# Turning gates in 32x32 blocks on VectorE, and slot sums over 32 tokens in sixteen parts of the array

## The chip, the cores and the metric

The kernel runs on one core of a Trainium2 chip. The metric is the device time of one execution, in microseconds, as the median of several runs. The core has TensorE (PE, matmuls into PSUM), VectorE (DVE), ScalarE (ACT), GpSimd (POOL) and SyncE (SP, which issues the DMAs).

## The reference

Three blocks follow each other. Talking-heads attention (4 batches, 12 heads, 448 tokens, 64 per head) gives `x` of 1792 tokens by 768. A feed-forward block with a gate follows, and a soft mixture of 8 experts with 4 slots each, 32 slots in all:

```
h = x @ w_in                    # 1792 x 2048
x = (h - tanh(h)) @ w_out       # the gated values g, then 1792 x 768
logits = x @ phi                # 1792 x 32
d = exp(logits - logits.max(0)); d /= d.sum(0) + 1e-09
slot_input = d.T @ x            # 32 x 768, then two matmuls per expert
...
c = exp(logits - logits.max(1)); c /= c.sum(1, keepdims=True) + 1e-09
out = c @ slot_out
```

## The kernel before

The kernel never forms `g @ w_out`. The logits are `g @ (w_out @ phi)`, with the product of the two weights (`wphi`) made once, and the slot inputs are `(d.T @ g) @ w_out`: a sum over tokens of `g`, 32 slots by 2048 features, which then goes through `w_out`. That sum over tokens is the place of the change.

The tokens come in four passes of 512, 512, 512 and 256 (`PASS`), the features in 16 blocks of 128, so there are 64 steps `t`, with `b, f = divmod(t, 16)`. A step computes one tile of `h` transposed, 128 features by 512 (or 256) tokens: 18 matmuls into one of three PSUM banks (`product`, L755), with the weights of `w_in` as the stationary side, split into a high and a low part. While TensorE computes step `t`, the other engines gate tile `t-1`: ScalarE squares it (`sq`), squares again (`qd`), takes tanh (`g`) and a mask (`mk`); VectorE forms `h - tanh(h)`, and where `h` is small replaces it by a polynomial in `qd` and `sq` (L786 to L800). `sq` lies in a PSUM bank.

The gated tile has features on the partitions. The sum over tokens needs tokens there, so TensorE turns it: `turn_g` (L826) makes four 128x128 transposes into PSUM, two steps after the product, and ScalarE copies the result (L829) into one of five SBUF buffers of 8 KB per partition (`tq`, `quad`). At the fourth to sixth step of the next pass, the softmax weights of the 32 slots for the pass (`et`, 32 slots in each of four copies) are turned in the same way (`slot_turn`, L946), and `slot_sum` (L958) contracts over 128 tokens at a time: 16 matmuls of 32 slots by 512 features, four of them side by side in the four 32-column parts of the array, half in one step and half in the next. A running sum `SA` (128 x 512) is rescaled and added to (L966).

Nothing is scheduled by a compiler. The order on each engine is the order in which the program issues instructions: `step` puts hooks between the matmuls of a product (`on(c, fn)` calls `fn` before the matmuls of contraction block `c`, `KD` after the last), and each engine goes through its own list in order, waiting on semaphores.

In the last pass the high part of a weight tile is made in two halves by VectorE (L714) and ScalarE (L716), and GpSimd subtracts it from the whole for the low part (L717). From the second pass on, SyncE loads expert weights (1536 KB each) into every buffer that comes free (`give`, `load_expert`). Behind the last step comes the tail: softmax and slot sum of the last pass, `dt` (L1152, the slot sums turned and scaled), `si` (times `w_out`, L1163), and the experts (`h`, `tz`, `so`).

Of the kernel before, what the change touches and what calls it, by code (L numbers as in the profile page):

```python
# [566 lines left out]
def moe_and_slots(tc, ident, xd, wi, wo, wo4, wis, consts, w1, w2, out, box):  # L567
# [23 lines left out]
    XW = KD * TM  # L591
    RU = 2 * DM
# [18 lines left out]
    def r32(ap):  # L611
        return ap.bitcast(F32R)
# [9 lines left out]
    quad, quad_a, quad_b = [xep.tile([128, FB * NRM], FP32, tag=f"quad{i}", name="quad") for i in range(3)]  # L622
# [120 lines left out]
    hps, quads, tok = {}, {}, {}  # L743
# [26 lines left out]
    def gate_act(t, beside=None):  # L770
        hp = hps[t]
        if t > 1:
            mem["sq"] = {t: bank(f"q{t % 2}", [128, PASS[t // NF]], "sq")}
        sq, qd, mk, g = temps_of(t)
        nc.scalar.activation(out=sq, in_=hp, func=ACTF.Square)  # L775
        nc.scalar.activation(out=qd, in_=sq, func=ACTF.Square, bias=tshift)
        if t >= LAST:
            gate_poly(t)
        if beside:
            beside()  # L780
        nc.scalar.activation(out=g, in_=hp, func=ACTF.Tanh)
        nc.scalar.activation(out=mk, in_=sq, func=ACTF.Relu, bias=tlimit, scale=-1.0)  # L782
# [6 lines left out]
    def gate_first(t):  # L789
        hp = hps[t]  # L790
        sq, qd, mk, g = temps_of(t)
        if t < LAST:
            gate_poly(t)
        nc.vector.tensor_tensor(out=g, in0=hp, in1=g, op=ALU.subtract)
# [17 lines left out]
    def turn_bank(shape, name):  # L812
        if mem.get("sum") is not None:
            return bank("r0", shape, name)
        turns[0] += 1
        return bank(f"r{turns[0] % 2}", shape, name)

    def turn_g(t):
        b, f = divmod(t, NF)
        n = blocks[b]  # L820
        if f % NG == 0:
            tok[b, f // NG] = place(b, f // NG)
        g = g_of(t)
        x = turn_bank([128, n, 128], "gt")
        for r in range(n):
            nc.tensor.transpose(out=x[:, r, :], in_=g[:, r * 128:(r + 1) * 128], identity=ident)  # L826
        i = f % NG
        dst = tok[b, f // NG].rearrange("p (r f) -> p r f", r=n)[:, :, i * 128:(i + 1) * 128]
        nc.scalar.activation(out=dst, in_=x, func=ACTF.Copy)  # L829

    def place(b, k):
        if b == NPASS - 1:
            n = blocks[b] * FB
            return quads["C" if k < 2 else "D"][:, k % 2 * n:(k % 2 + 1) * n]
        return quads["AECDB"[(b * NQ + k) % 5]]
# [105 lines left out]
    def slot_turn(b):  # L941
        a, et = es_in[b]
        n = blocks[b]
        xe = turn_bank([128, n, NSL], "etp")
        for r in range(n):
            nc.tensor.transpose(out=xe[:, r, :], in_=et[:NSL, r * 128:(r + 1) * 128], identity=ident[:NSL, :NSL])  # L946
        es = keep.tile([128, NRM, NSL], FP32, tag="es", name="es")
        nc.scalar.activation(out=es[:, :n], in_=xe, func=ACTF.Copy)
        es_in[b] = (a, es)

    def slot_sum(b, lo, hi):
        a, es = es_in[b]
        if lo == 0:
            mem["sum"] = bank("r1", [128, FB], "sp")
        x = mem["sum"]
        for r in range(lo, hi):
            for k in range(NQ):
# [3 lines left out]
        if hi < blocks[b]:  # L961
            return
        mem["sum"] = None
        s = mem["SA"][:, :FB]
        if b:
            nc.vector.scalar_tensor_tensor(out=s, in0=s, scalar=a, in1=x, op0=ALU.mult, op1=ALU.add)  # L966
        else:
            nc.vector.tensor_copy(out=s, in_=x)
# [7 lines left out]
    def step(t):  # L976
# [14 lines left out]
        if t > 2:  # L991
            split_half(t + 1, 0)
            gate_act(t - 1, lambda: split_half(t + 1, 1) if t >= NF else split_w(t + 1, nc.gpsimd))
        else:
            split_w(t + 1, nc.gpsimd)
# [6 lines left out]
        on(4 if t > LAST + 2 else 2, turn_g, u)  # L1002
# [98 lines left out]
    mem["mk"] = tmp.tile([128, TM], FP32, tag="mk", name="mk")  # L1101
    mem["wo"] = [mem["ex"][0][:, i * DM:(i + 1) * DM] for i in range(NG)]
# [3 lines left out]
    quads.update(A=quad_a, B=quad_b, C=tq[:, :FB * NRM], D=tq[:, FB * NRM:], E=quad)  # L1106
# [29 lines left out]
    give(tmp.tile([128, EXB], FP32, tag="tz", name="ex"))  # L1136
    mix_t(b)
# [11 lines left out]
    nc.vector.tensor_scalar(out=sr, in0=ident, scalar1=rv, scalar2=None, op0=ALU.mult)  # L1149
    dt = bank("h2", [128, NG, 128], "dt")  # L1150
# [256 lines left out]
```

## Time and profile before

| | |
|---|---|
| time, median of 3 runs | 930.33 us (929.08 to 930.88) |
| profiled execution | 929.89 us, of which the span of the trace is 928.2 us |
| mean granted TensorE clock | 0.988 of 2.4 GHz |
| busy: PE, DVE, ACT, POOL | 97%, 61%, 62%, 32% of the span |
| attention, then the 64 steps | to about 485 us, then to 818 us |
| tail | 818 to 928 us |

Busy shares are unions of the times in which an engine had an instruction. Matmuls overlap in the pipeline, so one lasts longer than the distance from its start to the next one's start. One FP32 matmul is recorded as two instructions (x2); a matmul on fp32r data (`hp`) or a transpose is one. The chain of waits follows the work that ended last back to the start, and what stands on it adds up to the span.

### The profile page before, as it was taken

The numbers are of one execution on the slowest core, as the hardware profiler recorded it, in microseconds if no ns is written. First come the engines' busy times: TensorE is split into PE (matmuls) and PEld (weight loads), VectorE is DVE, ScalarE is ACT, GpSimd is POOL, SyncE is SP. The second block draws the span as 40 slices with busy tenths as digits, with TensorE's granted clock in tenths as the row PEclk, the third lists the DMA queues.
The fourth block names the chain that finished last, engine by engine and source line by source line (L and its number), as shares of the span: only waits on it lengthen the run. The fifth ranks groups of instructions, "written<-read, shape, count | busy, mean of one in ns | idle before, by whom it ended". The sixth has DMA issues, their size and how long they took to land.

```text
span 928.2 us, 19426 instructions
## 1 busy us (share of the span) xinstructions
PE 898.9 (97%) x6926; PEld 659.8 (71%) x6926; DVE 564.2 (61%) x1267; ACT 574.0 (62%) x1299; POOL 296.5 (32%) x499
## 2 busy tenths in 40 slices
PE   8999999999999999999999999999999999999995
PEld 6667777777777777777777777767776776874542
DVE  3576667767577676786555567567766776740104
ACT  4776767777677777777666576646664665730113
POOL 1464445644456444565432222000000014610000
PEclk9999999999999999999999999999999999998997
DMA  6988688976889567674467868769764445879997
GB/s 134 241 219 234 190 242 226 235 216 200 230 233 267 179 201 215 205 249 145 144 238 246 324 232 269 257 243 365 290 226 157 155 131 187 314 297 425 422 389 279
DMA packets 143988, 223.95 MB, mean 241 GB/s; under 512 B 60756, under 2 KB 125332, under 8 KB 140052
## 3 DMA queue, kind: packets, MB, share of 16 engines
q1 hardware_dynamic: 140544, 209.83, 70.3%
q10 hardware_dynamic: 3348, 12.87, 3.6%
q8 instruction: 56, 0.92, 0.4%
q14 instruction: 40, 0.33, 0.1%
HBM read 147.96 MB, written 36.18 MB: 198 GB/s over the span
## 4 chain that ended last, share of the span: by engine, by line
PE 90%; DMA 3%; ACT 3%; DVE 2%; issue 1%; POOL 0%; ACTq 0%; POOLq 0%; SPq 0%; DVEq 0%
PE hp L755 24%; PE pm L297 15%; PE tm L333 14%; PE vx L357 8%; PE sc L266 7%; PE h L1195 3%; DMA D<-S 3%; PE gt L826 3%; PE so L1234 2%; PE tz L1213 2%; PE lgp L876 2%; PE sp L958 1%; PE wt L845 1%; PE qx L245 1%; PE wp L857 1%
## 5 line engine op out<-in xcount | busy, mean ns | idle before, releaser
L333 PEld LDWEIGHTS tm<-wk,e 120*112 120x112 f32 (+1 forms) x1440 | 174.0, 177 | 70.7 <-issue 58.9
L299 DVE TENSOR_REDUCE mx<-pm 120x1 f32<-120x448 f32 x180 | 111.9, 622 | 125.2 <-PE pm L297 124.6
L336 ACT ACTIVATE aT<-tm 112x480 f32<-112x480 f32 x180 | 105.4, 586 | 120.5 <-PE tm L333 120.5
L297 PE MATMUL pm<-D,wpre 120*120 120x448 f32 x360 | 174.2, 566 | 3.8 <-DMA D<-S 2.2
L333 PE MATMUL tm<-wk,e 120*112 120x120 f32 (+1 forms) x1440 | 176.7, 266 | 1.0 <-POOL wk L323 1.0
L323 POOL TENSOR_SCALAR wk<-wpost,rv 120x120 f32<-120x120 f32 x180 | 125.0, 695 | 136.2 <-PE tm L333 115.2
L755 PE MATMUL hp<-xa,rg 128*128 128x512 f32 x576 | 152.5, 405 | 0.0
L755 PEld LDWEIGHTS hp<-xa,rg 128*128 128x128 f32 x576 | 102.4, 188 | 28.5 <-issue 10.7
L306 ACT ACTIVATE e<-pm,mx 120x448 f32<-120x448 f32 x180 | 113.5, 631 | 4.9 <-DVE rv L318 2.3
L717 POOL TENSOR_TENSOR rg<-rg 128x384 fp32r<-128x384 f32 x32 | 32.0, 1013 | 207.9 <-DVE rg L714 193.8
L274 ACT ACTIVATE S<-sc 120x448 f32<-120x448 f32 (+1 forms) x186 | 90.7, 543 | 5.3 <-PE sc L266 3.0
L357 PE MATMUL vx<-aT,vn 112*64 112x120 f32 (+1 forms) x1536 | 84.0, 262 | 0.0
L786 DVE SCALAR_TENSOR_TENSOR qd<-qd,sq 128x512 f32<-128x512 f32 (+1 forms) x62 | 38.3, 617 | 71.6 <-ACT mk L782 63.5
L357 PEld LDWEIGHTS vx<-aT,vn 112*64 112x64 f32 x1536 | 73.9, 137 | 6.2 <-issue 1.1
L775 ACT ACTIVATE sq<-hp 128x512 f32<-128x512 f32 (+1 forms) x62 | 32.9, 530 | 72.6 <-PE hp L755 72.6
L755 PE MATMUL hp<-xb,rg 128*128 128x512 f32 x288 | 74.7, 404 | 0.0
L312 POOL TENSOR_SCALAR rv<-ss 120x1 f32<-120x1 f32 x180 | 43.0, 239 | 96.8 <-ACT e L306 84.6
L297 PEld LDWEIGHTS pm<-D,wpre 120*120 120x120 f32 x360 | 51.4, 182 | 26.4 <-issue 11.4
L266 PE MATMUL sc<-khi,qT 64*120 64x448 f32 (+1 forms) x384 | 68.8, 387 | 0.8 <-DVE qT L249 0.8
L68 POOL TENSOR_TENSOR fa<-fa,f 128x384 f32<-128x384 f32 x64 | 65.3, 1020 | 5.3 <-issue 0.3
L755 PEld LDWEIGHTS hp<-xb,rg 128*128 128x128 f32 x288 | 52.0, 188 | 16.6 <-issue 6.3
L708 POOL TENSOR_TENSOR rg<-rg 128x768 fp32r<-128x768 f32 x13 | 24.0, 1844 | 67.9 <-PE gt L826 33.5
(173 smaller groups left out, 1356.9 us busy)
## 6 DMA issues: line engine op xcount, KB each, us to landing
ex<-in_moe_w_dram SPq DMA_DIRECT2D x25, 1536.0 KB
D<-S SPq DMA_DIRECT2D x172, 210.0 KB
rg<-wis SPq DMA_DIRECT2D x32, 768.0 KB
f<-in_moe_w_in_dram SPq DMA_DIRECT2D x32, 384.0 KB
f<-in_moe_w_out_dram SPq DMA_DIRECT2D x32, 384.0 KB
wis<-rg ACTq DMA_DIRECT2D x16, 768.0 KB
rg<-wi SPq DMA_DIRECT2D x26, 384.0 KB
wi<-fa SPq DMA_DIRECT2D x32, 192.0 KB
```

The costliest lines, as they stand in the source:

```text
L68: eng.tensor_tensor(out=out, in0=bits(a), in1=bits(p), op=ALU.add)
L266: nc.tensor.matmul(xs[e][0][:ni], lhsT=qT[n][s, l, p, :ni], rhs=kt[s], start=(i == 0), stop=(i == 2))
L274: nc.scalar.activation(out=dst, in_=xs[e][0][:ni], func=ACTF.Copy)
L297: nc.tensor.matmul(x[:r], lhsT=wpre[:r, :m, :], rhs=D_t.pop(s)[:r], start=True, stop=True)
L299: nc.vector.tensor_reduce(out=mx[:r], in_=x[:r], op=ALU.max, axis=AX.X, negate=True)
L306: nc.scalar.activation(out=e[:r], in_=pp_t.pop(s)[:r], func=ACTF.Exp, bias=mx_t.pop(s)[:r], accum_out=ss[:r])
L312: nc.gpsimd.tensor_scalar(out=rv[:r], in0=ss_t.pop(s)[:r], scalar1=EPS, scalar2=None, op0=ALU.add)
L323: nc.gpsimd.tensor_scalar(out=wk[:r], in0=wpost[:r], scalar1=ss_t.pop(s)[:r], scalar2=None, op0=ALU.mult)
L333: nc.tensor.matmul(x[:, c, :, :m], lhsT=e[:r, c * JP:(c + 1) * JP], rhs=wk[:r, :, :m], start=True, stop=True)
L336: nc.scalar.activation(out=attn_t[n][:, :, :, c0:c0 + m], in_=x[:, :, :, :m], func=ACTF.Copy)
L357: nc.tensor.matmul(x[64 * e:64 * e + 64, i, :ni], lhsT=nat_v[b, h // NP][:, h % NP, c, :], rhs=a[:, c, h, :ni], start=(c == 0), stop=(c == ...
L755: nc.tensor.matmul(hp, lhsT=r32(w[:, m, hl, cs]), rhs=r32(x_of(b, c, l)), start=(c == 0 and i == 0), stop=(c == KD - 1 and i == 2))
```

## The change

`turn_g` no longer uses TensorE, PSUM and ScalarE. VectorE's block transpose turns each 32x32 block of the gated tile in place: partition 32i + l of block tb holds, after it, token 32 tb + l for the features 32i to 32i + 31 of the tile. A 512-token tile takes two instructions of 128x256, one into each of two buffers (`tq` and `th`, 16 KB per partition each, which hold a whole pass); a 256-token tile takes one. `et` is turned in one VectorE instruction.

`slot_sum` contracts over the 32 tokens of one block in one 32-partition group: 64 matmuls of 32x32 by 512 columns for a pass of 512 tokens. Partition group i (row part) goes into PSUM bank i, token block tb into partition group tb mod 4 (column part), so sixteen different parts of the array are named one after another. The four banks are added into `SA`, now 128 x 2048, by four VectorE instructions. `dt` takes 16 matmuls of 32 columns, which also add up the four token groups.

As the buffers hold one pass only, tiles of the next pass are turned after the slot sum: none in the third and fourth step of a pass, three in the fifth, one in every other; in the first pass five at the seventh step. The slot sum stands as a whole behind the fourth step. `sq` moves from two PSUM banks to one SBUF tile. The polynomial (`gate_poly`) is issued before tanh in all passes, not in the last alone. The high halves of the last pass's weights are both made by ScalarE. One of three late expert buffers (`z2`) is gone.

```
-            if m == 0:
-                nc.vector.tensor_copy(out=r32(h), in_=l)
-            else:
-                nc.scalar.activation(out=r32(h), in_=l, func=ACTF.Copy)
+            nc.scalar.activation(out=r32(h), in_=l, func=ACTF.Copy)
...
-            mem["sq"] = {t: bank(f"q{t % 2}", [128, PASS[t // NF]], "sq")}
+            mem["sq"] = {t: mem["sb"][:, :PASS[t // NF]]}
...
-        if t >= LAST:
-            gate_poly(t)
+        gate_poly(t)
...
     def turn_g(t):
         b, f = divmod(t, NF)
-        n = blocks[b]
...
-        for r in range(n):
-            nc.tensor.transpose(out=x[:, r, :], in_=g[:, r * 128:(r + 1) * 128], identity=ident)
...
-        nc.scalar.activation(out=dst, in_=x, func=ACTF.Copy)
+        g = g_of(t).rearrange("p (b l) -> p b l", l=NSL)
+        for part in range(0, PASS[b] // NSL, NTB // 2):
+            nc.vector.transpose(out=turned[part * 2 // NTB][:, :, f, :], in_=g[:, part:part + NTB // 2, :])
...
+        nc.vector.transpose(out=es, in_=et)
...
+    def slot_sum(b):
         a, es = es_in[b]
+        n = PASS[b] // NSL
+        xs = [bank(tag, [128, NF, NSL], "sp") for tag in ("q0", "q1", "r0", "r1")]
+        for tb in range(n):
+            g = tb % NG
+            rows = turned[tb * 2 // NTB][:, tb % (NTB // 2)]
+            for i in range(NG):
+                p = slice(NSL * i, NSL * i + NSL)
                 nc.tensor.matmul(
-                    x[NSL * k:NSL * k + NSL, :], lhsT=es[:, r, :], rhs=tok[b, k][:, r * FB:(r + 1) * FB],
-                    start=(r == 0), stop=(r == blocks[b] - 1))
+                    xs[i][NSL * g:NSL * g + NSL], lhsT=es[p, tb * NSL:(tb + 1) * NSL], rhs=rows[p],
+                    start=(tb < NG), stop=(tb >= n - NG))
+        sums = mem["SA"].rearrange("p (f i l) -> p i f l", i=NG, l=NSL)
+        for i in range(NG):
+            s = sums[:, i]
...
-        on(4 if t > LAST + 2 else 2, turn_g, u)
...
-            on(4, slot_turn, b - 1)
+            on(1, slot_turn, b - 1)
             on(KD, gates_last, b - 1)
-        if b and f in (4, 5):
-            on(3, slot_sum, b - 1, 2 * f - 8, 2 * f - 6)
+            on(KD, slot_sum, b - 1)
...
+        if b == 0 and f < 7:
+            if f == 6:
+                for i in (1, 0, 2, 3, 4):
+                    on(4, turn_g, i)
+        elif f < 2 or f > 4:
+            on(4, turn_g, u)
+        elif f == 4:
+            for i in range(3):
+                on(4, turn_g, t - 4 + i)
...
-    for i in range(NG):
+    for i in range(NF):
         nc.tensor.matmul(dt[:, i, :], lhsT=mem["SA"][:, i * 128:(i + 1) * 128], rhs=sr, start=True, stop=True)
```

What this moves on TensorE, before, in the fourth to seventh step of the second pass (`hp` a product, `gt` the turns, `sp` the slot sum):

```order
L755 MATMUL hp<-xb,rg 128x512 x12
L826 MATMUL gt<-ident,g 128x128 x4
L755 MATMUL hp<-xb,rg 128x512 x3
L958 MATMUL sp<-quad,es 32x512 x2
L958 MATMUL sp<-tq,es 32x512 x2
L958 MATMUL sp<-quad,es 32x512 x2
L958 MATMUL sp<-tq,es 32x512 x2
L755 MATMUL hp<-xb,rg 128x512 x15
L826 MATMUL gt<-ident,g 128x128 x4
```

And with the change, in the same steps and on to the logits (`lgp`):

```order
L754 MATMUL hp<-xb,rg 128x512 x27
L938 MATMUL sp<-tq,es 32x512 x32
L938 MATMUL sp<-th,es 32x512 x32
L754 MATMUL hp<-xb,rg 128x512 x36
L857 MATMUL lgp<-g,wphi 32x512 x4
```

The turns are gone from TensorE's list, and the slot sum is one run of 64 matmuls where two runs of 8 stood.

On VectorE, before, around the update of `SA` in the second pass (L786 and L787 the polynomial, L794 `h - tanh`, L799 and L800 the replacement):

```order
L786 SCALAR_TENSOR_TENSOR qd<-qd,sq 128x512
L787 SCALAR_TENSOR_TENSOR qd<-sq,qd 128x512
L794 TENSOR_TENSOR g<-hp,g 128x512
L968 COPY SA<-sp 128x512
L799 SCALAR_TENSOR_TENSOR hp<-qd,hp 128x512
L800 COPY_PREDICATED g<-mk,hp 128x512
```

And with the change, at the fourth and fifth step (L784 to L796 are the same five operations):

```order
L947 COPY SA<-sp 128x16x32 x4
L784 SCALAR_TENSOR_TENSOR qd<-qd,sq 128x512
L785 SCALAR_TENSOR_TENSOR qd<-sq,qd 128x512
L790 TENSOR_TENSOR g<-hp,g 128x512
L795 SCALAR_TENSOR_TENSOR hp<-qd,hp 128x512
L796 COPY_PREDICATED g<-mk,hp 128x512
L816 STREAM_TRANSPOSE tq<-g 128x8x32
L816 STREAM_TRANSPOSE th<-g 128x8x32
L816 STREAM_TRANSPOSE tq<-g 128x8x32
L816 STREAM_TRANSPOSE th<-g 128x8x32
L816 STREAM_TRANSPOSE tq<-g 128x8x32
L816 STREAM_TRANSPOSE th<-g 128x8x32
```

The update has become four, and six transposes stand behind the gate of the step; in the steps behind it there are two.

On ScalarE, before, one step late in the last pass (L775, L776 squares, L716 a weight half, L781 tanh, L782 the mask, L829 the copy of the turned gates):

```order
L775 ACTIVATE sq<-hp 128x256
L776 ACTIVATE qd<-sq,tshift 128x256
L716 ACTIVATE rg<-rg 128x384
L781 ACTIVATE g<-hp 128x256
L782 ACTIVATE mk<-sq,tlimit 128x256
L829 ACTIVATE tq<-gt 128x2x128
```

And with the change:

```order
L774 ACTIVATE sq<-hp 128x256
L775 ACTIVATE qd<-sq,tshift 128x256
L715 ACTIVATE rg<-rg 128x384 x2
L779 ACTIVATE g<-hp 128x256
L780 ACTIVATE mk<-sq,tlimit 128x256
```

The second weight half has come from VectorE, and the copy of the turned gates is gone.

## Rows read from the trace of the kernel before

**Rows 1.** The page: the chain by line; a product's row, busy us, mean ns.

```profile
PE hp L755 24%; PE pm L297 15%; PE tm L333 14%; PE vx L357 8%; PE sc L266 7%; PE h L1195 3%; DMA D<-S 3%; PE gt L826 3%; PE so L1234 2%; PE tz L1213 2%; PE lgp L876 2%; PE sp L958 1%; PE wt L845 1%; PE qx L245 1%; PE wp L857 1%
...
L755 PE MATMUL hp<-xa,rg 128*128 128x512 f32 x576 | 152.5, 405 | 0.0
```

**Rows 2.** Stretches: us, then busy us by engine (instructions), clock, DMA share, GB/s.

```profile
600.00:700.00 100.00, 99.58 (x505) 72.97 (x506) 68.77 (x119) 60.05 (x111) 0.00 (x0) 1.00 0.74 274
```

**Rows 3.** TensorE in order of time, second pass: start, us, line, count.

```profile
641.59 0.60 PE L826 MATMUL gt<-ident,g 128*128 128x128 f32 x4
...
642.73 2.02 PE L755 MATMUL hp<-xb,rg 128*128 128x512 f32 x8
...
647.41 0.60 PE L826 MATMUL gt<-ident,g 128*128 128x128 f32 x4
647.77 4.43 PE L755 MATMUL hp<-xb,rg 128*128 128x512 f32 x18
652.04 0.60 PE L826 MATMUL gt<-ident,g 128*128 128x128 f32 x4
```

**Rows 4.** VectorE in order of time, the same step.

```profile
647.42 0.69 DVE L786 SCALAR_TENSOR_TENSOR qd<-qd,sq 128x512 f32<-128x512 f32 x1 [0.66 <-ACT mk L782]
...
650.07 0.75 DVE L800 COPY_PREDICATED g<-mk,hp 128x512 f32<-128x512 int32 x1
650.70 0.68 DVE L741 TENSOR_TENSOR xa<-xa 128x512 fp32r<-128x512 f32 x1
```

**Rows 5.** TensorE in order of time: score products, and a slot sum.

```profile
306.48 0.37 PE L266 MATMUL sc<-klo,qT 64*88 64x448 f32 x2
306.68 0.57 PE L266 MATMUL sc<-khi,qT 64*88 64x448 f32 x4
...
780.45 0.60 PE L958 MATMUL sp<-quad,es 128*32 128x512 f32 x3
...
780.88 0.60 PE L958 MATMUL sp<-quad,es 128*32 128x512 f32 x3
```

**Rows 6.** VectorE's groups in the product stage: count, busy us, mean ns.

```profile
L741 DVE TENSOR_TENSOR xa<-xa 128x512 fp32r<-128x512 f32 x10 | 6.6, 681 | 1.2 <-ACT xa L740 1.1
...
L741 DVE TENSOR_TENSOR xc<-xc 128x256 fp32r<-128x256 f32 x6 | 2.5, 410 | 0.0
...
L867 DVE COPY wphi<-wq 128x128 f32<-128x128 f32 x4 | 1.2, 292 | 6.3 <-PE wq L865 6.3
```

**Rows 7.** Single lines: count, ns min/median/max, first and last start.

```profile
L57 DVE SCALAR_TENSOR_TENSOR fa<-f,fa x64: 535/548/1085, 40.8 to 446.0; 128x384 int32<-128x384 int32 x64
...
L323 POOL TENSOR_SCALAR wk<-wpost,rv x180: 586/593/1631, 25.3 to 482.2; 120x120 f32<-120x120 f32 x172, 108x120 f32<-108x120 f32 x8
...
L717 POOL TENSOR_TENSOR rg<-rg x22: 1003/1012/1021, 756.3 to 798.3; 128x384 fp32r<-128x384 f32 x22
```

**Rows 8.** The last pass: TensorE in time, its longest wait, a piece of the chain.

```profile
760.27 0.88 PE L755 MATMUL hp<-xc,rg 128*128 128x256 f32 x6
...
790.51 2.40 PE L755 MATMUL hp<-xc,rg 128*128 128x256 f32 x18
...
817.61 1.05 PE L1122 MATMUL warm<-ident 128*128 128x128 f32 x8
...
PE gt L826 <- DVE g L800: 2.2, 1, 2.2
...
801.63 7.04 DMA rg<-wi
```

**Rows 9.** The chain that ended last, tail: start, us, what, count.

```profile
827.34 0.75 DVE SA L966
...
828.73 1.16 PE dt L1152 x8
...
839.61 0.45 PE ln L893 x4
```

**Rows 10.** One stretch of the tail, columns as in rows 2.

```profile
860.00:870.00 10.00, 10.00 (x130) 5.38 (x122) 0.19 (x1) 0.60 (x1) 0.62 (x2) 1.00 1.01 424
```

More of the change, by code (lines that the diff above doesn't have):

```diff
@@ L591, in moe_and_slots @@
     XW = KD * TM
+    NTB = TM // NSL
     RU = 2 * DM
@@ L621, in moe_and_slots @@
     xbuf = {0: [xap.tile([128, XW], FP32, tag=f"x{l}", name="xa") for l in range(2)]}
-    quad, quad_a, quad_b = [xep.tile([128, FB * NRM], FP32, tag=f"quad{i}", name="quad") for i in range(3)]
+    turned = [None, xep.tile([128, NTB // 2, NF, NSL], FP32, tag="th", name="th")]
+    quad = turned[1].rearrange("p b f l -> p (b f l)")
     ring = [w.rearrange("p (m h i) -> p m h i", m=2, h=2) for w in (rg[:, :RU], rg[:, RU:], *rgs)]
@@ L812, in turn_bank @@
     def turn_bank(shape, name):
-        if mem.get("sum") is not None:
-            return bank("r0", shape, name)
         turns[0] += 1
@@ L942, in slot_turn @@
         a, et = es_in[b]
[L943 to L948, printed above, removed]
+        es = (mem["tz"] if b == NPASS - 1 else keep).tile(
+            [128, PASS[b]], FP32, tag="es" if b == NPASS - 1 else "lp", name="es")
+        nc.vector.transpose(out=es, in_=et)
         es_in[b] = (a, es)
-    def slot_sum(b, lo, hi):
+    def slot_sum(b):
         a, es = es_in[b]
[L953 to L957, printed above, removed]
-                nc.tensor.matmul(
-                    x[NSL * k:NSL * k + NSL, :], lhsT=es[:, r, :], rhs=tok[b, k][:, r * FB:(r + 1) * FB],
-                    start=(r == 0), stop=(r == blocks[b] - 1))
[L961 to L968, printed above, removed]
+        n = PASS[b] // NSL
[5 more added lines that the diff above has]
+                p = slice(NSL * i, NSL * i + NSL)
+                nc.tensor.matmul(
+                    xs[i][NSL * g:NSL * g + NSL], lhsT=es[p, tb * NSL:(tb + 1) * NSL], rhs=rows[p],
[3 more added lines that the diff above has]
+            s = sums[:, i]
+            if b:
+                nc.vector.scalar_tensor_tensor(out=s, in0=s, scalar=a, in1=xs[i], op0=ALU.mult, op1=ALU.add)
+            else:
+                nc.vector.tensor_copy(out=s, in_=xs[i])
     pieces, folds = {}, {5: 0, 9: 1, 13: 2, 16: 3}
@@ L1046, in step @@
                 zp = whole.enter_context(tc.tile_pool(name="m_z", bufs=1, reuse_waits="tile"))
-                for i in range(3):
+                for i in range(2):
                     give(zp.tile([128, EXB], FP32, tag=f"z{i}", name="ex"))
@@ L1091, in moe_and_slots @@
     mem["thp"] = thp
-    tq = mids.tile([128, 2 * FB * NRM], FP32, tag="tq", name="tq")
+    tq = mids.tile([128, NTB // 2 * NF * NSL], FP32, tag="tq", name="tq")
+    turned[0] = tq.rearrange("p (b f l) -> p b f l", f=NF, l=NSL)
     xbuf[1] = [thp.tile([128, XW], FP32, tag=f"x{l}", name="xb") for l in range(2)]
-    mem["SA"] = mids.tile([128, FB], FP32, tag="SA", name="SA")
+    mem["SA"] = mids.tile([128, NF * 128], FP32, tag="SA", name="SA")
     mem["ex"] = [mids.tile([128, EXB], FP32, tag=f"ex{i}", name="ex") for i in range(NX)]
@@ L1101, in moe_and_slots @@
     mem["mk"] = tmp.tile([128, TM], FP32, tag="mk", name="mk")
+    mem["sb"] = tmp.tile([128, TM], FP32, tag="sq", name="sq")
     mem["wo"] = [mem["ex"][0][:, i * DM:(i + 1) * DM] for i in range(NG)]
@@ L1142, in moe_and_slots @@
     slot_run(b)
-    slot_sum(b, 0, blocks[b])
+    slot_sum(b)
     warm(3)
-    sr = keep.tile([128, 128], FP32, tag="et", name="sr")
+    sr = keep.tile([128, NSL], FP32, tag="et", name="sr")
     rv = keep.tile([128, 1], FP32, tag="rv", name="rv")
@@ L1148, in moe_and_slots @@
     nc.vector.reciprocal(out=rv, in_=rv)
-    nc.vector.tensor_scalar(out=sr, in0=ident, scalar1=rv, scalar2=None, op0=ALU.mult)
-    dt = bank("h2", [128, NG, 128], "dt")
-    for i in range(NG):
+    nc.vector.tensor_scalar(out=sr, in0=seld, scalar1=rv, scalar2=None, op0=ALU.mult)
+    dt = bank("h2", [128, NF, NSL], "dt")
+    for i in range(NF):
         nc.tensor.matmul(dt[:, i, :], lhsT=mem["SA"][:, i * 128:(i + 1) * 128], rhs=sr, start=True, stop=True)
@@ L1154, in moe_and_slots @@
     give(tq[:, 1024:])
-    dgT = wphi.rearrange("p (i k) s -> p i (k s)", i=NG)
-    nc.scalar.activation(out=dgT[:, :2], in_=dt[:, :2], func=ACTF.Copy)
-    nc.vector.tensor_copy(out=dgT[:, 2:], in_=dt[:, 2:])
+    dgT = wphi
+    nc.scalar.activation(out=dgT[:, :NF // 2], in_=dt[:, :NF // 2], func=ACTF.Copy)
+    nc.vector.tensor_copy(out=dgT[:, NF // 2:], in_=dt[:, NF // 2:])
     si = [bank(f"r{hf}", [128, HALF], "si") for hf in range(2)]
```

24 lines of the change are left out of this document (5 added, 19 removed).

## The prediction

> **What bounds the kernel now.** I read the chain of waits on the page first, then the busy times by stretch, then TensorE in order of time, and then the engine that is to take over the work. `hp` (L755), the first products, are the largest item of the chain that ended last, and `gt` (L826), the turning of the gates, stands on it with 3% of the span, as TensorE time [rows 1]. In the product stage TensorE has 99.6 of 100 us, VectorE 69, ScalarE 60, GpSimd nothing [rows 2]. So until about 760 us what is taken off TensorE comes off the span, as long as VectorE, which gets the work, does not become later than TensorE.
>
> What a turn costs TensorE is read from one step of the second pass. Eight undisturbed products of 512 columns take 2.02 us [rows 3]; one lasts 0.40 us [rows 1], so they start (2.02 - 0.40) / 7 = 0.231 us apart. From one `gt` to the next, with 18 products and no logits between, it is 652.04 - 647.41 = 4.63 us [rows 3]. 18 x 0.231 = 4.16, so a turn costs 4.63 - 4.16 = 0.47 us, more than its four transposes alone, since the first products behind it start late.
>
> **Part 1: gates off TensorE.** 48 turns of 512 tokens (three passes of 16 steps) x 0.47 = 22.5 us. The 16 turns of the last pass are not counted here: another engine sets the pace there (part 4). I take 22.
>
> **Part 2: gates onto VectorE.** Each 512-token tile is two block transposes of 128x256, 48 x 2 + 16 = 112 in all. No row of before shows this operation. The nearest is VectorE's 128x256 two-input operation, 0.41 us; the bounds are 0.29 us (a 128x128 copy) and 0.68 us (twice the elements) [rows 6]. I take 0.41. VectorE's five gate operations, from L786 to what follows L800, take 650.70 - 647.42 = 3.28 us without a wait among them; 0.66 us before them it waited for L782, which is not an input of L786 [rows 4]. The polynomial now stands ahead of tanh, so it starts when `qd` is there and this wait goes. A step becomes 3.28 + 0.82 = 4.10 us, or 4.8 us in the 6 of 16 steps that split `x` (0.68 us, rows 6), against TensorE's 4.16 us plus, every fourth step, logits. Over a pass that is 16 x 4.10 + 6 x 0.68 + about 6 us for softmax pieces and slot sums = 76 us for VectorE, and for TensorE 16 x 4.16 + 4 x 1.2 (the step with logits, 647.41 - 641.59 = 5.82 us, is 1.2 longer, rows 3) + 3.4 for the slot sum + about 1.5 for `lT` and `ln` = 76 us. That is level: VectorE is nearly as full as TensorE. Nothing is queued on TensorE for a turned tile until the slot sum, and a product writes over the accumulator of three steps before, so VectorE may run late unseen: a tile's gate ends about 1.3 (two squares) + 3.28 us after its product, its accumulator is wanted two steps, 8.5 us, after it, which leaves about 4. The bursts (10 transposes at the seventh step, 6 behind each slot sum) fit in that. I take 1.5 us for short stalls, range 0 to 4. At 0.29 us a transpose it is nothing; at 0.68 us see the rivals.
>
> **Part 3: the slot sums.** Before, instructions on four 32-column parts go abreast, and the next four start 0.43 us later [rows 5]: 32 / 4 x 0.43 = 3.4 us a pass, in two interruptions. After, 64 matmuls (128 instructions) on sixteen parts: 128 / 16 x 0.43 = 3.4 us, in one interruption. That column parts run abreast is in the rows (three entries in 0.60 us together); that row parts do is in the score products, which use 64 rows each: from one pair of 448 columns to the next it is 0.20 us, and one alone needs 448 / 512 x 0.231 = 0.20 [rows 5]. Four row parts at once no row shows. Bounds: 3.4 us, or, if only column parts overlap, 128 / 4 x 0.43 = 13.8 us. I take 3.4, the value that both rows point to: change 0, and nothing for the `etp` transposes that go.
>
> VectorE has four 128x512 updates of `SA` where it had one, 0.75 us each [rows 9]; in passes 0 to 2 they are in the 6 us above. At the end they are on the path.
>
> **Part 4: the last pass,** from 760.27 to 817.61 us, 57.3 us for 16 products of 256 columns [rows 8]. It is not TensorE's work that fills it. Two things lie ahead of it that go: the transposes wait up to 2.2 us for VectorE (L800), and later the chain lies 7.04 us in a weight DMA [rows 8]. With no turn in its queue TensorE goes on two products further until a free accumulator stops it. One thing comes. `sq` lies in SBUF, so both polynomial operations read two operands there, and GpSimd's two weight subtractions per step (1.01 us each) do too. In the attention stage that combination collides: L57, a VectorE operation on two SBUF operands, takes 0.55 us, and up to 1.09; GpSimd's L323 takes 0.59, and up to 1.63 [rows 7]. So each waits for the other. GpSimd's 2 x 1.01 us and VectorE's 2 x 0.41 us [rows 6, 7] per step then stand in line: 2.9 us per step, where 18 products and a turn had taken about 2.4 [rows 8]. The copy that VectorE made for the split moves to ScalarE, which loses the eviction of `gt` for it, so ScalarE is as full as before. 14 steps x 2.9 + 3 for the sum + about 7 until the third product (the last 512-token tile must first pass through ScalarE's squares and VectorE's 3.28 us, behind the tile before it) = 51 us, 6 less than 57.3; were the two to alternate in the worst way (VectorE idle between its two, 3.35 us), 57. I take -4, range -9 to +2.
>
> The Trainium skill, page "SBUF — State Buffer", section "SBUF: two separate sides", says that GpSimd shares a port pair with VectorE operations that have two SBUF inputs, that it is an exclusive lock, and that the loser blocks for the whole instruction. It speaks against putting `sq` into SBUF. By it alone, without what the trace shows of the waits that go, the last pass would be 14 x (2.9 - 2.4) = 7 us longer; the stretched maxima of L57 and L323 agree with it.
>
> **Part 5: the tail.** Three more `SA` updates: 3 x 0.75 = 2.2 us. `dt` becomes 16 matmuls of 32 columns instead of 4 of 128: 32 instructions. `ln`, the same form, took 0.45 us for 4, so 32 x 0.11 = 3.6 against 1.16, +2.4 (by dt's own spacing, 1.16 / 8, +3.5) [rows 9]. Sum 4.6; I take +4.5, range +2 to +6. One expert buffer fewer is loaded in the last pass, so one more 1536 KB load falls behind 818 us, where DMA runs at 424 GB/s with its engines full [rows 10]: 1.57 MB / 424 = 3.7 us later for the last loads. TensorE itself comes 4.5 us later there, so I count 0 (up to +3).
>
> **Sum**, against the profiled execution (929.89 us, span 928.2 and 1.7 around it): -22 + 1.5 - 4 + 4.5 = -20, so 909.9. The median of the runs is 0.44 above the profiled execution: 910.
>
> **Rivals.**
> 1. *Column parts alone overlap* (the slower side). Place: the slot sums on TensorE, at the fourth step of a pass. Price: 13.8 - 3.4 = 10.4 us x 3, and half of it at the end, 36 us: 946. It decides once a sum takes more than about 9 us, that is with fewer than six or seven parts at once. For it: no row with four row parts. Against it: row pairs and column fours overlap. 7%.
> 2. *VectorE becomes the bound.* With 0.68 us a transpose, a pass is 76 + 32 x 0.27 = 85 us against 76; pass 0, with more on TensorE, hides it, the other two pay 8 to 9 each: about +16, so 926. For it: both sums are level. Against it: nothing but the assumed duration. 13%.
> 3. *The lock sets the last pass* (the page's rule and the 3.35 us alternation, with the DMA wait still there): part 4 becomes +3 to +7, 917 to 921. For it: 2.9 us per step is already more than the products. Against it: the old pass took 57.3 us, far more than 16 x 2.4 = 38, so it has waits to lose. 17%.
> 4. *The turns were cheaper than they look,* because products behind them would have started late anyway (weights, not columns): 0.36 us instead of 0.47, the distance from 647.41 to 647.77, gives 17 instead of 22: 915. This lies inside the forecast's range.
>
> **How the numbers follow.** Forecast (904 to 917): 57%. Rival 1 7%, rival 2 13%, rival 3 17%; 6% are left for a last pass that gains all 9 us and no short stalls (below 904). The 80% range leaves out rival 1 and a little of the low end: 903 to 927. A measurement of this kernel can tell 0.2%, 1.9 us, from no change. Slower by that: rival 1 and the far end of rival 2, 10%; within it 5%; faster 85%.
>
> **What would show it.** Right: in passes 0 to 2 the products of one step follow the last without a break, a step without logits takes 4.2 us; the slot sum is 128 entries in about 3.7 us; a block transpose takes 0.41 us; L784 and L785 in the last pass, or GpSimd beside them, show maxima well above 0.42 and 1.02 us; four `SA` updates in a row and a `dt` of 3.6 us near the end. Wrong: TensorE waiting for VectorE in the second or third pass; a slot sum of 7 us or more; a last pass over 57 us; TensorE waiting for a DMA behind 890 us.

## The result, and the profile after

The kernel after takes 935.9 us (median of 14 runs, 930.53 to 942.56) against 929.2 for the kernel before on the same chip: a ratio of 1.0074, 95% interval 1.0056 to 1.0092. It is slower by 0.7%, where 2% faster was predicted. The profiled execution took 934.47 us, with a span of 932.6.

The stages show where. The table has the time from the first product (`hp`) of a pass to the first of the next, read from TensorE's records in order of time; the last two columns run from the first to the last product of the last pass, and from there to the end of the span.

| us | up to the products | pass 1 | pass 2 | pass 3 | last pass | tail | span |
|---|---|---|---|---|---|---|---|
| before | 482.7 | 102.8 | 89.6 | 85.2 | 57.2 | 110.7 | 928.2 |
| after | 484.0 | 104.2 | 82.4 | 77.7 | 62.6 | 121.7 | 932.6 |
| difference | +1.3 | +1.4 | -7.2 | -7.4 | +5.3 | +11.0 | +4.4 |
| predicted | 0 | -6.8 | -6.8 | -6.8 | -4 | +4.5 | -20 |

(Passes are numbered from one here; of the prediction's -22 and +1.5 us a third stands in each of the first three.) The second and third pass gained what was predicted. The first gained nothing, the last lost, and the tail lost more than twice the forecast. What stands ahead of the products is outside the change; it took 481.9 to 486.8 us in the twelve profiles of this document, so the +1.3 there says nothing.

The page of the kernel after: busy time by engine, then the chain that ended last, by line. It answers to [rows 1].

```profile
PE 883.6 (95%) x7048; PEld 648.2 (70%) x7048; DVE 623.5 (67%) x1379; ACT 554.7 (59%) x1247; POOL 305.9 (33%) x499
...
PE hp L754 17%; PE pm L297 15%; PE tm L333 15%; PE vx L357 8%; PE sc L266 7%; DMA D<-S 2%; PE h L1182 2%; DVE qd L785 2%; PE so L1221 2%; PE sp L938 2%; DMA ex<-in_moe_w_dram 2%; DVE qd L784 2%; PE lgp L857 1%; PE tz L1200 1%; DVE g L790 1%
```

Products hold 17% of the chain where they held 24%, and in their place stand the polynomial (`qd`, L784 and L785, which are L786 and L787 of before; 36 us where they had 2.8), other gate operations of VectorE, which had hardly a part in it, and a DMA of expert weights, which had none.

The same stretch as in [rows 2], and one in the tail, by stretches:

```profile
600.00:700.00 100.00, 98.43 (x659) 72.67 (x659) 86.12 (x165) 51.81 (x91) 0.00 (x0) 1.00 0.74 286
828.00:838.00 10.00, 10.00 (x84) 6.10 (x83) 0.55 (x2) 0.38 (x1) 0.00 (x0) 0.70 0.27 82
```

In the middle passes VectorE rose from 69 to 86 us in 100 and TensorE still has 98: the work moved, and TensorE hardly waits for it. In the tail, 17 to 27 us behind the last product, the DMA engines are at 0.27 of their time, with a granted clock of 0.70. The kernel before has them full from 828 us on, as in [rows 10].

TensorE in order of time, kernel after: a slot sum in the second pass, and a stretch of products that answers to [rows 3].

```profile
612.27 2.31 PE L938 MATMUL sp<-tq,es 32*32 32x512 f32 x62 [0.55 <-DVE es L926]
...
614.22 2.50 PE L938 MATMUL sp<-th,es 32*32 32x512 f32 x63
616.66 3.52 PE L754 MATMUL hp<-xb,rg 128*128 128x512 f32 x14
```
```profile
654.72 6.44 PE L754 MATMUL hp<-xb,rg 128*128 128x512 f32 x27
```

27 products of a step and a half follow each other with nothing between, where [rows 3] had a turn every 18. The slot sum runs from 612.27 to 616.66, 4.39 us for its 128 instructions.

In the first pass, the groups of VectorE and GpSimd and the wait that TensorE had not had before (groups; then waits: us, times, longest):

```profile
L710 POOL TENSOR_TENSOR rg<-rg 128x768 fp32r<-128x768 f32 x13 | 28.6, 2201 | 66.3 <-ACT rg L709 50.7 <-DMA ex<-wo 15.6
...
L785 DVE SCALAR_TENSOR_TENSOR qd<-sq,qd 128x512 f32<-128x512 f32 x13 | 13.6, 1045 | 0.4
L784 DVE SCALAR_TENSOR_TENSOR qd<-qd,sq 128x512 f32<-128x512 f32 x13 | 12.2, 935 | 9.0 <-ACT qd L775 9.0
```
```profile
PE wp L838 <- DVE ex L832: 6.0, 2, 3.1
```

And the same two operations in the second and third pass, where GpSimd has next to nothing to do:

```profile
L785 DVE SCALAR_TENSOR_TENSOR qd<-sq,qd 128x512 f32<-128x512 f32 x32 | 22.8, 714 | 1.1
L784 DVE SCALAR_TENSOR_TENSOR qd<-qd,sq 128x512 f32<-128x512 f32 x32 | 21.6, 676 | 7.6 <-ACT qd L775 7.6
```

Same operation, same shapes, same buffers: 0.71 and 0.68 us alone, 1.05 and 0.94 beside GpSimd's weight subtractions (L710). The chain in the first pass shows what this did, in order of time (start, us, what):

```profile
530.37 2.22 DVE qd L785
532.59 0.47 DVE ex L832
...
536.37 2.22 DVE qd L785
538.59 0.47 DVE ex L832
...
544.60 0.69 DVE qd L785
545.29 0.48 DVE ex L832
545.82 0.62 PE wp L838
```

A polynomial operation of 0.69 us takes 2.22; the copy of turned weights (`ex`, L832) is queued behind it; and the fold of the weights on TensorE (`wp`) waits for that copy.

### The profile page after: what moved, and what is told of

It is laid out like the page before. It is cut to its first block, busy times and chain, and to the rows that moved or that the text cites. A ratio compares the mean times of both kernels' runs of the same rounds, so it can differ in the third digit from the quotient of the medians.

```text
span 932.6 us, 19813 instructions
## 1 busy us (share of the span) xinstructions
PE 883.6 (95%) x7048; PEld 648.2 (70%) x7048; DVE 623.5 (67%) x1379; ACT 554.7 (59%) x1247; POOL 305.9 (33%) x499
## 4 chain that ended last, share of the span: by engine, by line
PE 78%; DVE 11%; DMA 6%; ACT 3%; issue 2%; POOL 0%; SPq 0%; DVEq 0%; ACTq 0%; POOLq 0%
PE hp L754 17%; PE pm L297 15%; PE tm L333 15%; PE vx L357 8%; PE sc L266 7%; DMA D<-S 2%; PE h L1182 2%; DVE qd L785 2%; PE so L1221 2%; PE sp L938 2%; DMA ex<-in_moe_w_dram 2%; DVE qd L784 2%; PE lgp L857 1%; PE tz L1200 1%; DVE g L790 1%
## 5 line engine op out<-in xcount | busy, mean ns | idle before, releaser
L754 PE MATMUL hp<-xa,rg 128*128 128x512 f32 x576 | 144.2, 399 | 0.4 <-POOL rg L710 0.4
L754 PEld LDWEIGHTS hp<-xa,rg 128*128 128x128 f32 x576 | 104.7, 188 | 30.5 <-issue 9.9
L716 POOL TENSOR_TENSOR rg<-rg 128x384 fp32r<-128x384 f32 x32 | 36.2, 1151 | 193.5 <-ACT rg L715 182.1
L754 PE MATMUL hp<-xb,rg 128*128 128x512 f32 x288 | 70.3, 399 | 0.0
L784 DVE SCALAR_TENSOR_TENSOR qd<-qd,sq 128x512 f32<-128x512 f32 (+1 forms) x62 | 42.9, 692 | 17.8 <-ACT qd L775 17.8
L785 DVE SCALAR_TENSOR_TENSOR qd<-sq,qd 128x512 f32<-128x512 f32 (+1 forms) x62 | 52.2, 842 | 2.1
```

The lines of the kernel that those rows point to most:

```text
L754: nc.tensor.matmul(hp, lhsT=r32(w[:, m, hl, cs]), rhs=r32(x_of(b, c, l)), start=(c == 0 and i == 0), stop=(c == KD - 1 and i == 2))
L785: nc.vector.scalar_tensor_tensor(out=qd, in0=sq, scalar=-TG_A, in1=qd, op0=ALU.add, op1=ALU.mult)
```

## The experiments

Times of the stages, as in the table above, from the profiled execution of each:

| us | pass 1 | pass 2 | pass 3 | last pass | tail | median |
|---|---|---|---|---|---|---|
| after | 104.2 | 82.4 | 77.7 | 62.6 | 121.7 | 935.9 |
| 1 `sq` in PSUM | 96.5 | 82.4 | 77.7 | 56.7 | 120.0 | 920.5 |
| 2 late polynomial | 105.3 | 82.3 | 77.7 | 63.3 | 121.7 | 934.2 |
| 3 30 idle matmuls | 109.8 | 82.4 | 77.7 | 63.7 | 121.4 | 936.8 |
| 4 before, two buffers | 102.7 | 89.6 | 85.2 | 55.1 | 114.0 | 931.8 |
| 5 14 idle matmuls | 108.5 | 82.4 | 77.7 | 62.4 | 121.2 | 937.7 |
| 6 1 and 5 | 96.5 | 82.3 | 77.7 | 57.4 | 118.0 | 918.4 |
| 7 two halves of `sq` | 105.8 | 82.4 | 77.7 | 57.5 | 123.0 | 933.4 |
| 8 6, later sum | 96.6 | 82.4 | 77.7 | 56.3 | 115.9 | 917.0 |
| 9 8, copy on VectorE | 96.5 | 82.3 | 77.7 | 60.0 | 117.4 | 919.4 |
| 10 8, other order | 96.5 | 82.4 | 77.7 | 59.2 | 117.6 | 917.8 |

The kernel before had medians of 928.7 to 928.8 beside them.

### 1. sq in PSUM where GpSimd works

```
-            mem["sq"] = {t: mem["sb"][:, :PASS[t // NF]]}
+            if t < NF or t >= LAST and not 2 <= t % NF <= 4:
+                mem["sq"] = {t: bank(f"q{t % 2}", [128, PASS[t // NF]], "sq")}
+            else:
+                mem["sq"] = {t: mem["sb"][:, :PASS[t // NF]]}
```

> The kernel after, with `sq` again in a PSUM bank in the first pass and in the last one (not in steps 2 to 4 of the last, where the slot sum has the banks). Theory 'lock': two SBUF operands are what stretches the second polynomial operation and GpSimd's subtractions; then L785's successor in the last pass falls from 1.13 us to about 0.43, GpSimd's subtractions from 1.15 to about 1.0 us (last pass) and from 2.20 to about 1.85 us (first pass), the last pass from 62.6 to 54-58 us, the first from 104.2 to 99-102, and the kernel from 936 to 922-929. Rival 'amount': it is VectorE's added transposes and their place, not the lock; then durations fall but both passes stay within 1.5 us of 104.2 and 62.6, and the kernel stays at 934-937.

Measured: 920.5 us, 0.9911 of before (0.9877 to 0.9944): this one edit turns a slower kernel into a faster one. Groups of its first pass (L787 and L788 are the polynomial here, L841 the fold):

```profile
L710 POOL TENSOR_TENSOR rg<-rg 128x768 fp32r<-128x768 f32 x13 | 24.0, 1847 | 62.6 <-ACT rg L709 57.6 <-DMA wis<-rg 5.0
...
L788 DVE SCALAR_TENSOR_TENSOR qd<-sq,qd 128x512 f32<-128x512 f32 x13 | 9.0, 691 | 0.5
...
L787 DVE SCALAR_TENSOR_TENSOR qd<-qd,sq 128x512 f32<-128x512 f32 x13 | 8.8, 679 | 8.4 <-ACT qd L778 8.4
...
L841 PE MATMUL wp<-ex,SA 128*32 128x512 f32 x36 | 5.8, 598 | 0.0
```

Both polynomial operations are back at 0.68 to 0.69 us, GpSimd at 1.85, and the fold waits for nothing. The first pass takes 96.5 us, 6.3 under before: the gain that was predicted and missing. The burst of ten transposes at its seventh step and the early polynomial are still there, so they were not the cause by themselves. The edit also gives `sq` two buffers again. In the first pass of after, ScalarE's square had waited only 2.2 us for the one buffer, and in the second and third pass, where GpSimd rests, one buffer costs nothing; but no run parts the two in the first pass. In the last pass GpSimd's subtractions fell only from 1.15 to 1.05 us and the pass by 5.9 us; experiment 7 parts that.

### 2. The polynomial of the first pass behind tanh again

```
-        gate_poly(t)                       # in gate_act
+        if t >= NF:
+            gate_poly(t)
...
+        if t < NF:                         # in gate_first
+            gate_poly(t)
```

> The kernel after, with the polynomial of the first pass behind tanh again, so that VectorE's copies of turned weights stand ahead of it. Theory 'queue': the interruption for each fold of the weights fell behind because VectorE's copies wait in the queue behind a polynomial that waits for ScalarE and GpSimd; then the fold's four interruptions go from 3.7 us back to about 2.2, the first pass from 104.2 to 97-100, the kernel from 936 to 929-932. Rival 'lock' for the first pass: VectorE is late because its two-operand instructions wait for GpSimd; then the interruptions stay above 3 us, the pass stays within 1.5 us of 104.2, and the kernel at 934-937.

Measured: 934.2 us, first pass 105.3. The order theory falls. TensorE's wait at the fold went from 6.0 to 0.9 us, and came back a little further down its list, as a wait for the folded weights' copy (waits of its first pass):

```profile
PE lgp L860 <- DVE wphi L851: 6.8, 3, 4.2
```

VectorE is late whatever its order; only what is queued behind it changes.

### 3 and 5. Idle matmuls between the last slot sum and dt

```
     slot_sum(b)
-    warm(3)
+    warm(30)        # experiment 3; 14 in experiment 5
```

> The kernel after, with 30 idle matmuls instead of 3 behind the last slot sum, to span the four updates of SA. Theory 'clock': TensorE's 2.4 us of idleness ahead of dt let the clock fall to 1.2 GHz and doubled dt (7.0 us); then dt takes 3.4-3.7 us, what is behind it starts 3.5 us earlier, the expert loads too, and the kernel goes from 936 to 931-933. Rival 'loads': the end hangs on the last expert loads alone, which queue for bandwidth; then dt is short but TensorE waits longer for the last weights, and the kernel stays at 934-937.

> The kernel after, with 14 idle matmuls instead of 3 behind the last slot sum: 14 x 0.22 us = 3.1 us, which ends when the updates of SA do, where the 30 before outlasted them by 3.4 us. Theory 'clock': dt takes 3.6 us instead of 7.0, the last si product ends 3.4 us earlier, and the kernel goes from 936 to 931-933. Rival 'loads': dt is short, but the end moves less than 1 us, since the expert loads end when they ended, 934-937.

`dt` and what is ahead of it in the tail, from the chains of after, 3, 5 and 8 in turn:

```profile
818.65 2.35 PE sp L938 x62
821.00 2.70 DVE SA L945 x4
824.30 7.04 PE dt L1139 x32
```
```profile
833.96 3.49 PE dt L1139 x32
```
```profile
829.19 4.38 PE dt L1139 x32
834.58 7.46 PE si L1150 x64
```
```profile
812.14 3.74 PE dt L1145 x32
816.40 5.31 PE si L1156 x64
```

In after TensorE was granted 0.50 (1.2 GHz) over the whole of `dt`, having been busy 1.86 of the 4 us ahead of it; in 8 it was granted 1.00 (2.4 GHz) there:

```profile
824.00:831.40 7.40, 7.10 (x33) 7.11 (x34) 0.24 (x1) 0.03 (x1) 0.00 (x0) 0.50 0.53 218
820.00:824.00 4.00, 1.86 (x38) 0.83 (x16) 2.95 (x6) 0.00 (x0) 0.00 (x0) 0.96 1.03 410
```
```profile
812.00:816.00 4.00, 4.00 (x36) 3.88 (x35) 0.06 (x1) 0.09 (x1) 0.00 (x0) 1.00 0.98 409
```

So `dt` takes 3.5 to 3.7 us at 2.4 GHz, as predicted (3.6), and 7.04 at 1.2. That much of 'clock' holds. As a cure both runs failed: with 30 idle matmuls `dt` began 3.4 us later behind the last product than in after, which gave back what they saved; with 14 the granted clock fell to 0.50 a little later, from 832.1 to 838.9 us, at the end of `dt` and in `si` (7.46 us). Neither made the kernel faster. Their profiles also have a first pass of 109.8 and 108.5 us: with `sq` in SBUF it ranged from 104.2 to 109.8 in five profiles, in PSUM from 96.5 to 96.6 in five, so a total on top of the SBUF version tells little of 3 us.

### 4. The kernel before with two expert buffers

```
-                for i in range(3):
+                for i in range(2):
                     give(zp.tile([128, EXB], FP32, tag=f"z{i}", name="ex"))
```

> The kernel before, with two expert buffers instead of three where its first pool closes; nothing else is changed. Theory 'buffer': the 1536 KB that are loaded later push the last load back by 3.7 us (1.57 MB at 424 GB/s), and TensorE, which does not wait for weights there before, waits 2-4 us: 931-933. Rival 'hidden': the load is hidden, as the prediction had it: 929-930, with no wait of TensorE for a load near the end.

Measured: 931.8 us, ratio 1.0032 (1.0013 to 1.0050). The tail is 3.3 us longer, and a load is on the chain, which it was not before; the kernel after has the same piece:

```profile
890.52 17.25 DMA ex<-in_moe_w_dram
```
```profile
893.14 17.19 DMA ex<-in_moe_w_dram
```

The theory holds: the load was not hidden.

### 6. Both cures

> `sq` in PSUM in the first and last pass, and 14 idle matmuls behind the last slot sum. Theory: lock and clock add up, because they sit in different stages: dt goes from 5.1 to 3.6 us, 920.5 - 1.5 to -3 = 917-919. Rival 'loads': the tail is as long as without the idle matmuls, 920-922.

Measured: 918.4 us, 0.9897 (0.9864 to 0.9930), with `dt` at 4.07 us and the tail 2 us shorter than in experiment 1. The intervals of 1 and 6 overlap, so only the sum of the two is shown, not what the idle matmuls add.

### 7. Two halves of sq in the last pass

```
-            mem["sq"] = {t: mem["sb"][:, :PASS[t // NF]]}
+            n = PASS[t // NF]
+            i = t % 2 * n if t >= LAST else 0
+            mem["sq"] = {t: mem["sb"][:, i:i + n]}
```

> The kernel after, with `sq` of the last pass in the two halves of its SBUF tile by turns. It tells the lock from the one buffer, which the return to PSUM took away together. Rival 'one buffer': ScalarE's square waited 15 us for the polynomial, because there is one sq; with two this wait falls below 5 us and the last pass goes from 62.6 to 57-60, the kernel to 930-933. Theory 'lock': the wait moves elsewhere, the polynomial's second operation still takes 0.9-1.2 us and GpSimd's subtractions 1.15, the last pass is 61-64 and the kernel 934-937.

Last pass of after (groups), then of this kernel:

```profile
L716 POOL TENSOR_TENSOR rg<-rg 128x384 fp32r<-128x384 f32 x31 | 35.1, 1152 | 27.4 <-ACT rg L715 15.9 <-PE lgp L857 8.3 <-PE hp L754 3.1
...
L785 DVE SCALAR_TENSOR_TENSOR qd<-sq,qd 128x256 f32<-128x256 f32 x15 | 14.0, 934 | 0.5
...
L774 ACT ACTIVATE sq<-hp 128x256 f32<-128x256 f32 x15 | 5.8, 384 | 16.2 <-DVE qd L785 14.7 <-PE hp L754 1.1 <-PE lgp L857 0.4
```
```profile
L716 POOL TENSOR_TENSOR rg<-rg 128x384 fp32r<-128x384 f32 x31 | 32.7, 1076 | 24.5 <-ACT rg L715 22.5 <-PE hp L754 2.0
L786 DVE SCALAR_TENSOR_TENSOR qd<-qd,sq 128x256 f32<-128x256 f32 x14 | 10.6, 754 | 1.6 <-ACT qd L777 1.6
L787 DVE SCALAR_TENSOR_TENSOR qd<-sq,qd 128x256 f32<-128x256 f32 x14 | 8.0, 575 | 0.5
L776 ACT ACTIVATE sq<-hp 128x256 f32<-128x256 f32 x15 | 5.5, 369 | 8.4 <-PE hp L754 6.8 <-DVE qd L787 1.6
```

The lock is still there: the polynomial takes 0.75 + 0.58 us where it took 0.42 + 0.42 in the kernel before (last pass, groups):

```profile
L787 DVE SCALAR_TENSOR_TENSOR qd<-sq,qd 128x256 f32<-128x256 f32 x15 | 6.4, 424 | 0.5
L786 DVE SCALAR_TENSOR_TENSOR qd<-qd,sq 128x256 f32<-128x256 f32 x15 | 6.3, 418 | 7.6 <-ACT qd L776 7.4
```

But ScalarE's wait for the polynomial falls from 14.7 to 1.6 us, and the last pass from 62.6 to 57.5 us, almost what PSUM gave. The four profiles with one `sq` there have 62.4 to 63.7 us, the six with two 56.3 to 60.0. So in the last pass it was the one buffer that let the lock reach TensorE: a late polynomial held the next square, and with it all that is queued behind the square on ScalarE. (That the copies for GpSimd are what passed it on to the products is read from the waits, and no run shows it by itself.) Here the rival was right. The kernel gained less than the pass (933.4 us); its other stages were 1.6 us (first pass) and 1.3 us (tail) longer in the profile.

Part of the 5.1 us came with the clock. In after the granted clock was 0.50 for 6.8 us of the last pass, in two stretches; ahead of the first TensorE had waited 4.6 us for the turned weights of the slot sum (`es`), and the sum then took 5.9 us instead of 4.4. Here it was 0.50 for 3.4 us. The last pass of after, of 1 and of 10, by stretches (the clock is the third figure from the end):

```profile
748.00:811.00 63.00, 52.14 (x461) 42.22 (x461) 55.46 (x115) 40.39 (x99) 34.49 (x31) 0.95 0.54 183
```
```profile
743.00:800.00 57.00, 48.54 (x460) 39.70 (x459) 49.10 (x117) 38.81 (x98) 31.54 (x31) 1.00 0.59 202
```
```profile
739.00:799.00 60.00, 51.95 (x464) 41.72 (x464) 48.89 (x117) 39.59 (x100) 31.25 (x31) 0.94 0.57 192
```

Experiment 10 has two buffers, 6.8 us at 0.50 like after, and a last pass of 59.2 us. At a like clock one buffer therefore costs some 3 to 4.5 us, as far as single profiles can tell.

### 8. The slot sum inside the last pass, one step later

(To experiment 6; `sq` now lies in SBUF in steps 2 to 5 of the last pass.)

```
-            on(KD, slot_sum, b - 1)                     # at f == 3
+            if t < LAST:
+                on(KD, slot_sum, b - 1)
+        if t >= LAST and f == 4:
+            on(KD, slot_sum, b - 1)
...
-        elif f == 4:
+        elif f == 4 + (t >= LAST):                      # and four tiles turned there
```

> As the version with sq in PSUM and 14 idle matmuls, and the slot sum inside the last pass (that of the pass before it) one step later, so that the turned exponentials are ready when TensorE comes to it; the tiles of four steps instead of three are turned behind it. Theory 'es': 7.5 us of interruption hold about 2.8 us of products and 4.7 of waiting for the turned exponentials; the interruption falls to 3-4 us and the last pass from 56.7 to 52-55, the kernel to 913-916. Rival 'pace': another engine sets the pace of these steps, TensorE waits the same time a little later, the pass stays at 56-58, the kernel at 917-920.

In after TensorE stood 4.6 us ahead of this sum (waits of its last pass):

```profile
PE sp L938 <- DVE es L926: 4.6, 1, 4.6
```

Measured: 917.0 us, 0.9876 of before (0.9838 to 0.9914), the lowest median of all, and under both kernels; its interval overlaps those of 1, 6, 9 and 10. The interruption of the products fell from 6.5 to 4.6 us against experiment 6, but the pass only from 57.4 to 56.3: 'pace' is nearer than 'es', though 1 us is less than a last pass varies by (next experiment). The tail is 2.1 us shorter than in 6 (115.9 us): this run kept 2.4 GHz through `dt` and `si`, which the same 14 idle matmuls did not do in 5.

### 9 and 10. Who paces the last pass, and the order of the sum

```
-            nc.scalar.activation(out=r32(h), in_=l, func=ACTF.Copy)
+            if m == 0:                                  # experiment 9, split_half
+                nc.vector.tensor_copy(out=r32(h), in_=l)
+            else:
+                nc.scalar.activation(out=r32(h), in_=l, func=ACTF.Copy)
```
```
-        for tb in range(n):                             # experiment 10, slot_sum
-            for i in range(NG):
+        for j in range(n * NG):
+            tb, i = j // 16 * NG + j % NG, j // NG % NG
...
```

> The version with sq in PSUM, 14 idle matmuls and the later slot sum, with the first copy of each weight half in the last pass on VectorE again, as before the change. Theory 'ScalarE paces': with both copies ScalarE has about 2.7 us of work in a step of the last pass, and GpSimd waited 22 us for its copies; with one copy less (0.51 us) that wait halves and the last pass goes from 56.3 to 52-55, the kernel from 917 to 912-915. Rival 'VectorE paces': VectorE, which turns the gates now, has 2.5 us of its own and gets 0.36 more; GpSimd then waits for VectorE instead, the last pass is 56-59 and the kernel 916-920.

> The same version, with the matmuls of the slot sums in another order: four column parts of one row part after another, where the four row parts of one column part followed each other. The sum took 5.6 us for 128 instructions, 0.70 us for sixteen parts, where 0.43 was predicted. Theory 'order': parts that follow one another share the column part and so get in each other's way; with the other order a sum takes 3.4-4.5 us, 1-2 us less three times over, 913-915. Rival 'streams': sixteen parts at once cost 0.70 us in whatever order, 5.4-5.8 us, and the kernel stays at 916-918.

Experiment 9: 919.4 us, last pass 60.0. GpSimd's wait moved from ScalarE to VectorE (waits of 8, then of 9):

```profile
POOL rg L716 <- ACT rg L715: 22.1, 13, 4.2
```
```profile
POOL rg L719 <- DVE rg L716: 12.3, 10, 2.3
```

The rival fits, but 10, which leaves the last pass as it is in 8 but for the order of one sum, has 59.2 there, so 2 to 3 us of a last pass vary from one execution to the next, and 9 shows no more than that the copy's move is no gain. Part of that is the clock again: in the last pass of 8 the granted clock was 1.00 throughout, in 9 it was 0.50 for 3.4 us, in 10 for 6.8. What sets a last pass of some 57 us, before and after, stays open.

Experiment 10: 917.8 us. The sum of the second pass, TensorE in order of time:

```profile
603.26 2.31 PE L941 MATMUL sp<-tq,es 32*32 32x512 f32 x62 [0.53 <-DVE es L929]
...
605.22 2.50 PE L941 MATMUL sp<-th,es 32*32 32x512 f32 x63
607.65 6.57 PE L754 MATMUL hp<-xb,rg 128*128 128x512 f32 x27
```

From 603.26 to 607.65 is 4.39 us, as in after. The order makes no difference. (The 5.6 us and 0.70 us of the expectation count from one product to the next, with the wait for `es` and a product's own time; the sum itself is 4.39, or 0.55 for sixteen parts.)

## Why the prediction was wrong

**Part 1, gates off TensorE: right where nothing else came.** -7.2 and -7.4 us in the second and third pass, for 16 turns each at the 0.47 us that the step gave. In the first the same gain shows as soon as `sq` is back in PSUM (-6.3).

**Part 2, gates onto VectorE: the first of three steps that failed.** Its 0.41 us for a block transpose held (0.39 to 0.45), and VectorE kept up in the second and third pass (busy 72 and 70 us of 82 and 78, where the prediction had 76 of 76). But it priced the first pass with the polynomial at 0.69 us and said that VectorE may run late unseen. The lock was looked for in the last pass alone, although GpSimd subtracts weights in the first as well, 13 times 1.85 us. There VectorE has a consumer that cannot wait: the copies of turned weights, queued behind the polynomial. "Nothing is queued on TensorE for a turned tile" was true and not enough, since other work passes through the same queue. Price: 104.2 - 96.5 = 7.7 us (experiment 1, with the second buffer that came back with it). The page's rule in the prediction ("SBUF — State Buffer", "SBUF: two separate sides", the Trainium skill) agrees with the trace here: 0.69 us became 2.22, which is 1.53 more and less than the 1.85 of a whole subtraction.

**Part 3, the slot sums: mechanism right, size off.** Sixteen parts do overlap; a sum takes 4.4 us, not 3.4, three times over. The Trainium skill, page "TensorE: Matmul & The Clock Gate", section "Measured speedup vs the span model", gives 10.6 for sixteen such parts, not 16; an estimate by it is 128 x 0.43 / 10.6 = 5.2 us. The measured time lies between that and the forecast (a factor of 12.5). Rival 1 is out.

**Part 4, the last pass: +5.3 for -4, the second step that failed.** The lock was seen, and the 2.9 us per step came out (3.0 without the interruption), but by luck: with `sq` in PSUM in most steps a step still takes 2.8 (experiment 1), so the lock alone does not set it. Two other terms of the sum were too small. "3 for the sum" was 10.8 us between products (4.6 of waiting for `es`, 5.9 of sum at a clock that fell); the sum had no wait for `es` in it. "About 7 until the third product" was 9.4. What the prediction also left out is that `sq` had become one buffer where it was two banks, so that a late polynomial holds ScalarE. Two halves, at no cost in space, give back 5.1 us, a part of it by the clock. Even with two buffers the interruption was 6.9 us (experiment 7) and the pass not shorter than before, so -4 was wrong by about that much on its own; of the two waits that were to go, the one for a weight DMA stayed (6.55 us on the chain of after, 7.04 before). Rival 3 had the right place and its +3 to +7 the right size, but put it down to the lock alone.

**Part 5, the tail: +11.0 for +4.5, the third step that failed.** The last `si` product ends 27.6 us after the last `hp`, where it ended 18.7 after: the updates of `SA` took 2.70 us for 0.75, about as predicted; `dt` took 7.04, not 3.6, because it ran at 1.2 GHz, of which the prediction said nothing. The remaining 2.1 us are put down to the buffer that was counted at 0: alone it costs 3.3 us of tail in experiment 4, the far end of the range that was given (up to +3). Where the clock stayed at 2.4 GHz through `dt` and `si` (experiment 8), the tail is 5.2 us longer than before, near the forecast with the buffer in it. A late `si` also gives its buffers back late, so the DMA engines that were full in [rows 10] stood at 0.27 from 828 to 838 us.

**The sum.** From -20 to +4.4 in the span is 24.4 us: the first pass 8.2, the last 9.3, the tail 6.5, the time ahead of the products 1.3, less 0.9 that the second and third gained over the forecast.

## What to carry to other kernels

Before an operand moves from PSUM to SBUF, list every stretch in which GpSimd works, not only the one that comes to mind, and for each what is queued behind the lengthened instruction and who waits for it. When a buffer moves, count its copies: two banks that become one tile turn a neighbour's delay into one's own. Where the tail is a row of loads, a buffer given up and a TensorE that comes late to release the others both land on the end of the kernel, whatever was saved before.

## What the runs showed of the hardware

- A VectorE operation on two SBUF operands of 512 columns took 0.69 us alone and up to 2.31 beside a GpSimd subtraction on SBUF of 1.85 us, which itself took up to 2.35; with one operand in PSUM neither changed.
- With this contention the first pass took 104.2, 105.3, 105.8, 108.5 and 109.8 us in five profiles, and the granted clock was 0.50 for 0, 3.4, 3.4, 10.2 and 13.7 us of it. TensorE had been busy 9.0 of the 11 us ahead of the longest of these stretches. With `sq` in PSUM the pass took 96.5 to 96.6 us in five profiles, at 1.00 throughout.
- Block transposes on VectorE, 128x256 from SBUF to SBUF, took 0.39 to 0.45 us, as long as a two-input operation of that size. In the first pass of after all but one ran between the subtractions; in the last pass of experiment 9 twelve ran mostly while GpSimd subtracted and took 0.40 to 0.44.
